# Scaled value copies of an attention kernel: made once per layer and loaded again, instead of made in every unit

## The chip, the cores and the metric

The kernel runs on one core of one Trainium2 chip. The metric is the time of one execution on the device in microseconds (us), as the median of several runs. The engines are called PE (matrix multiplication), ACT, DVE and POOL; SP issues the transfers between DRAM and the on-chip memory. PEld is the loading of weights into PE, which overlaps the matmuls.

## The reference

The program is a four-layer transformer stack on 2048 tokens of width 512: attention, MLP, attention, MLP, with the same weights in both attentions and in both MLPs. Attention has 32 heads of width 16.

```python
def _A_ref(x, wqkv, wo):                      # H = 32, Dh = 16
    q, k, v = split(x @ wqkv)
    p = softmax(einsum("bhqd,bhkd->bhqk", q, k) * Dh ** -0.5)
    return einsum("bhqk,bhkd->bhqd", p, v).merge_heads() @ wo
def _B_ref(x, w1, b1, w2, b2):                # F = 1376
    return gelu(layernorm(x) @ w1 + b1) @ w2 + b2
x = A_x
x = x + _A_ref(layernorm(x), A_wqkv, A_wo)
x = x + _B_ref(layernorm(x), B_w1, B_b1, B_w2, B_b2)
x = x + _A_ref(layernorm(x), A_wqkv, A_wo)
x = x + _B_ref(layernorm(x), B_w1, B_b1, B_w2, B_b2)
```

Everything is bfloat16 at the boundary.

## The kernel before

**Segments.** The code numbers the two attention layers L = 1 and L = 3. A layer is cut into units of 512 queries (in L = 3 the last unit is cut in two of 256), and a unit into 8 head groups (`hg`) of 4 heads. One unit and one head group make a *segment*; a segment's keys and values are 16 blocks of 128 tokens. The first unit of a layer starts before all keys are there, so its segments exist twice, as part 0 and part 1 (`nparts == 2`): key blocks 0 to 3 and 4 to 15 in L = 1, 0 to 11 and 12 to 15 in L = 3. All later units have `nparts == 1` and see all 16 blocks. That makes 32 segments with two parts and 56 with one, 88 in all.

**Two ways to an exponential.** A score tile is 128 keys by 512 queries, made on PE by `score` (L1354). In the usual way ACT takes two or three tiles at once from PSUM and writes their exponentials to `PT` (L1339). For the key blocks in `DK = (3, 6, 9, 12, 15)` there is a second way, the *d tile*: DVE copies the scores to 16-bit integers whose bits are read as bfloat16, an approximate exponential (L1431, `d_load`), and then makes three copies of two such tiles at a time, shifted by 32, 64 and 96 (L1462, `job_d`). The four versions are multiplied with four differently scaled versions of the values, so that the errors of the approximation average out. The scaled values are `vs`, three copies of the value blocks multiplied by `WSHIFT[1..3]`; the fourth is the unscaled `V`. So an ACT tile costs one value matmul on PE (L1528) and a d tile costs four. A value matmul has 17 columns (16 values and a one for the softmax's denominator); four heads run side by side in PE's columns.

**Where vs comes from.** `vs` has three slots. A segment takes a slot together with its query slot (`qt`, three of them), and once its queries are scaled (L1116, `job_qt`) `job_vs` is started. It has POOL multiply the segment's value blocks by the three constants, three instructions in a row (L1131), and then marks the blocks as usable. `take_d` gives out a d tile only when its block is marked. The slot is free again once the value matmuls of the segment that had it are done.

**Who decides the order.** The program is written out by a list scheduler in Python: jobs are generators that hand over tasks with a priority, and the scheduler keeps a modelled time for each engine and each resource and gives each engine the task that can start first. The model's durations stand in the code (the last numbers of each `I(...)`). The result is one fixed instruction list per engine, with semaphore waits between them. Whether a score tile goes to ACT or DVE is decided while this list is made: `take_d` gives a tile to DVE when DVE's modelled backlog and the free PSUM banks allow, and the others go to ACT. At the end `refill` puts matmuls with zeros into PE's modelled gaps (L1263, L1265, L1267). All transfers are issued on SP, in the order of its list, each with its own waits: the transposed load of a segment's queries (`qraw`, L1103), the transposes of the layernormed rows (`xnT`, `yT`) and of the attention output (`OT`), weights and stores.

**The side work.** Between the segments' instructions lie those of the layernorms, projections and MLPs of other units (`job_lnqkv`, `job_post`, `job_ffn`); POOL computes the inverse roots of the layernorms and merges the two parts of a split segment.

Of the kernel before, what the change touches and what calls it, by code (L numbers as in the profile page):

```python
# [8 lines left out]
BF16 = mybir.dt.bfloat16  # L9
# [29 lines left out]
DK = (3, 6, 9, 12, 15)  # L39
# [458 lines left out]
class Builder:  # L498
# [16 lines left out]
    def build_segments(self):  # L515
        self.segs = []
        four = [tuple(range(4 * c, 4 * c + 4)) for c in range(self.NC)]
        self.units = {1: four, 3: four[:3] + [four[3][:2], four[3][2:]]}
        for L in (1, 3):
            parts = [tuple(range(0, 4)), tuple(range(4, 16))] if L == 1 else [tuple(range(0, 12)), tuple(range(12, 16))]  # L520
            for pi in range(2):
                for hg in range(8):
                    self.segs.append(dict(L=L, qc=0, hg=hg, part=pi, nparts=2, kbs=parts[pi]))
            for qc in range(1, len(self.units[L])):
                for hg in range(8):
                    self.segs.append(dict(L=L, qc=qc, hg=hg, part=1, nparts=1, kbs=tuple(range(16))))
        for i, sg in enumerate(self.segs):
            sg["i"] = i
            sg["toks"] = self.units[sg["L"]][sg["qc"]]
            sg["W"] = 128 * len(sg["toks"])  # L530
            g = 512 // sg["W"]
            sg["dks"] = [kb for kb in sg["kbs"] if kb in DK]
            kbs = list(sg["kbs"]) if g == 1 else [kb for kb in sg["kbs"] if kb not in DK] + sg["dks"]
            sg["tiles"] = [(tuple(kbs[k:k + g]), hp) for k in range(0, len(kbs), g) for hp in range(4)]
            sg["nt"] = sg["n"] = len(sg["tiles"])
            sg["todo"] = [j for j, t in enumerate(sg["tiles"]) if not set(t[0]) <= set(DK)]
            sg["todod"] = [j for j, t in enumerate(sg["tiles"]) if set(t[0]) <= set(DK)]
            sg["rdy"] = []
            sg["sub"] = 0
            sg["emitted"] = 0  # L540
            sg["first"] = set()

    def alloc(self, es):
        nc = self.nc
        S, NT, NC, NFC = self.S, self.NT, self.NC, self.NFC
        t = lambda name, shape, dt: es.enter_context(nc.sbuf_tensor(name, shape, dt))
        self.xres = t("xres", [128, NT, 512], BF16)
        self.wqkv = t("wqkv", [128, 4, 1536], BF16)
        self.wo = t("wo", [128, 4, 512], BF16)
        self.wf = t("wf", [128, NFC, 512], BF16)  # L550
        self.bst = t("bst", [32, 128], BF16)
        self.b1c = t("b1c", [128, NFC], F32)
        self.ident = t("ident", [128, 128], BF16)
        self.zw = t("zw", [128, FILL_MOST], BF16)
        self.iog = t("iog", [128, 4], F32)
        self.iogt = t("iogt", [128, 4], F32)
        self.ioe = t("ioe", [32, 8, 4], F32)
        self.mask8 = t("mask8", [32, 8], F32)
        self.m4 = t("m4", [32, 4], F32)
        self.sel = t("sel", [32, 128], BF16)  # L560
        self.onesm = t("onesm", [128, 1], F32)
        self.row16 = t("row16", [128, 1], F32)
        self.qbias = t("qbias", [128, 1], F32)
        self.cneg = t("cneg", [128, 4], F32)
        self.chalf = t("chalf", [128, 1], F32)
        self.xnT = t("xnT", [128, 3, 4, 128], BF16)
        self.qk = t("qk", [128, 2, 2, 1024], BF16)
        self.vst = t("vst", [128, 1, 544], BF16)
        self.KT = t("KT", [128, 8, S], BF16)
        self.V = t("V", [128, 8, NT, 4, 17], BF16)  # L570
        self.qraw = t("qraw", [128, 2, 512], BF16)
        self.QT = t("QT", [128, 3, 512], BF16)
        self.PT = t("PT", [128, 23, 512], BF16)
        self.dp = t("dp", [128, NDP, 1024], U16)
        self.vs = t("vs", [128, 3, 3, len(DK), 68], BF16)
        self.OT = t("OT", [128, 8, 512], BF16)
        self.accT = t("accT", [128, 2, 512], F32)
        self.ob = t("ob", [128, 16, 8, 16], BF16)
        self.obl = t("obl", [128, 256], BF16)
        self.rv = t("rv", [128, 2, 16], F32)  # L580
        self.rowA = t("rowA", [128, 8, 16], BF16)
        self.dw = t("dw", [128, 2, 16], F32)
        self.den = t("den", [128, 8, 16], F32)
        self.yT = t("yT", [128, 4, 512], BF16)
        self.h16 = t("h16", [128, NFC, 512], BF16)
        self.g10 = t("g10", [128, 512], BF16)
        self.xn = t("xn", [128, 3, 512], BF16)
        self.sq0 = t("sq", [128, 1024], BF16)
        self.n2 = t("n2", [128, 4, 32], F32)
        self.n2k = t("n2k", [128, NT + 1, 32], BF16)  # L590
        self.nm = t("nm", [128, 32], BF16)
        self.qy = t("qy", [128, 4, 32], I32)
        self.qt1 = t("qt1", [128, 4, 32], F32)
        self.qt2 = t("qt2", [128, 4, 32], F32)
        self.kmx = t("kmx", [32, 4], F32)
        self.krhs = t("krhs", [32, 8], BF16)
        self.scl = t("scl", [128, 4, 8], F32)
        self.st = t("st", [128, 8, 6], F32)
        self.mv = t("mv", [128, 16, 2], F32)
        self.rs = t("rs", [128, 16], F32)  # L600
        self.ioi = self.dp[:, 6, 0:256].bitcast(F32)
        self.gv = self.h16[:, :, :].rearrange("p f n -> p (f n)")
        self.sbuf_left = nc.sbuf_bytes_remaining
        self.ps = es.enter_context(nc.psum_tensor("ps", [128, 8, 512], F32))
        self.q_scr = nc.dram_tensor("q_scr", [2, S, 1024], BF16, kind="Internal").ap()
        self.k_scr = nc.dram_tensor("k_scr", [S, 1024], BF16, kind="Internal").ap()
        self.v_scr = nc.dram_tensor("v_scr", [S, 544], BF16, kind="Internal").ap()
        self.sems = {}
        for e in list(ENGINES) + ["dma%d" % i for i in range(NDMAQ)]:
            self.sems[e] = es.enter_context(nc.semaphore("s_" + e))  # L610
        pl = self.S_.pools
        pl["mb"] = Pool([7, 5, 4, 3, 2, 1, 0])
        pl["pt3"] = Pool([0, 3, 6, 13, 18])
        pl["pt2"] = Pool([9, 11, 16, 21])
        pl["dp"] = Pool(range(8))
        pl["qraw"] = Pool(range(2))
        pl["qt"] = Pool(range(3))
        pl["qk"] = Pool(range(3))
        pl["vst"] = Pool([])
        pl["xn"] = Pool(range(3))  # L620
        pl["xnT"] = Pool(range(3))
        pl["sq"] = Pool(range(4))
        pl["n2"] = Pool(range(4))
        pl["accT"] = Pool(range(2))
        pl["st"] = Pool(range(8))
        pl["lnc"] = Pool(range(4))
        pl["kmx"] = Pool(range(1))
# [498 lines left out]
    def job_vs(self, sg, i, kbs):  # L1126

        q, hg, n = sg["qslot"], sg["hg"], len(kbs)
        yield ("keys", self.kv_keys(sg, kbs))
        src = self.V[:, hg, kbs[0]:kbs[-1] + 1:3, :, :].rearrange("p k h d -> p k (h d)")  # L1130
        yield Task("pool", 0.8, [I(lambda e, k=k: e.tensor_scalar(out=self.vs[:, q, k - 1, i:i + n, :], in0=src, scalar1=WSHIFT[k], scalar2=None, op0=ALU.mult),  # L1131
                                   [("V", hg, kb) for kb in kbs], [("vs", q, i + k2) for k2 in range(n)], 0.209 + 0.17 * n, [("vs", q, i + k2) for k2 in range(n)] if k > 1 else []) for k in (1, 2, 3)])
        for kb in kbs:
            self.S_.mark(("vs", sg["i"], kb))

    def job_kload(self, hg):

# [316 lines left out]
    def job_d(self, bt):  # L1454
# [4 lines left out]
        for k in range(1, len(SHIFT)):  # L1459
            v = yield ("get", "dp", sg["i"])  # L1460
            pr = 0.15 if not self.left(sg) and sg is self.segs[self.acc_seg] else 0.5 if self.left(sg) < DURGE else 2.5
            yield Task("dve", pr, [I(lambda e, k=k, v=v: e.tensor_scalar(out=self.dp[:, v, 0:N], in0=self.dp[:, u, 0:N], scalar1=float(SHIFT[k]), scalar2=None, op0=ALU.add),  # L1462
                                     [("dp", u, w) for w in range(n)], [("dp", v, w) for w in range(n)] + self.dres(v), 0.163 + 0.2605e-3 * N)])
            self.d_ready(bt, k, v, range(n))
        self.flying -= 1
        self.use_done(("dp", u))
# [12 lines left out]
    def try_pv(self):  # L1479
        S_ = self.S_  # L1480
        while True:
# [35 lines left out]
            for (s_, j, res, ap, use, sh) in pick:  # L1517
# [3 lines left out]
                sg["first"].add(hp)  # L1521
                for i, kb in enumerate(kbs):
                    if sh:
                        d = sg["dks"].index(kb)
                        v, RV = self.vs[:, q, sh - 1, d, 17 * hp:17 * hp + 17], ("vs", q, d)
                    else:
                        v, RV = self.V[:, hg, kb, hp, :], ("V", hg, kb)
# [361 lines left out]
```

## Time and profile before

| | |
|---|---|
| median of 5 runs | 1620.59 us (1618.09 to 1621.5) |
| profiled execution, its own time | 1618.09 us |
| its span (first to last instruction) | 1616.3 us |
| PE, ACT, DVE, POOL busy | 1577.8, 1548.3, 1471.6, 380.6 us |
| L1339, exponentials on ACT | 1470.0 us |
| L1431 and L1462, d tiles on DVE | 600.1 and 527.8 us |
| L1131, scaled values on POOL | 242.9 us in 240 instructions |

A row of the groups names the line, the engine, the operation, what it writes and reads, and the count; then its busy time and the mean duration of one in ns; then the idle time of the engine just before these instructions and what ended most of it. Busy time counts what overlaps once, so it can be less than count times mean. The chain that ended last is followed back from the last instruction, at each step to what released it. Matmuls are pipelined and their ends are modelled, so that a busy PE is not a PE at its peak.

### The profile page before, as it was taken

Reading aid. Unit: us, or ns where it says so; the run is one execution under the profiler, and the core shown is the slowest. Engines: PE = TensorE matmul, PEld = TensorE weight load, DVE = VectorE, ACT = ScalarE, POOL = GpSimd, SP = SyncE. Lnnn points to the kernel's source line nnn. Section 1 sums busy time; section 2 is a strip of 40 time slices with the busy share of each in tenths; the row PEclk is TensorE's granted clock in tenths of the full one; section 3 lists DMA queues with packets and bytes.
Section 4 is the critical chain, followed back from the end, with each engine's and each line's share of the span. In section 5 each row is a group of like instructions: output and inputs, shape, how many; then the busy total and the mean of one; then the engine's idle time right before and its main releaser. Section 6 shows DMA issues by size and latency. Waiting matters only on the chain.

```text
span 1616.3 us, 38868 instructions
## 1 busy us (share of the span) xinstructions
PE 1577.8 (98%) x16349; PEld 482.4 (30%) x16349; DVE 1471.6 (91%) x3249; ACT 1548.3 (96%) x1375; POOL 380.6 (24%) x574
## 2 busy tenths in 40 slices
PE   9999999999999999999999999999999999999998
PEld 3222222222222222232222222222222222344454
DVE  7899999989998899989999899999889979999794
ACT  6999999999999999999999989999999999999996
POOL 4354241011211121112111135511111101223210
PEclk9999999999999999999999999999999999999999
DMA  6651001102211221222722230100001000100100
GB/s 175 118 125 61 9 11 24 44 14 62 77 31 30 52 67 28 50 45 76 123 38 54 59 89 21 31 19 8 14 11 21 21 16 4 20 20 7 27 11 21
DMA packets 196849, 69.98 MB, mean 43 GB/s; under 512 B 176412, under 2 KB 191041, under 8 KB 196673
## 3 DMA queue, kind: packets, MB, share of 16 engines
q1 hardware_dynamic: 196672, 67.49, 18.8%
q8 instruction: 128, 2.10, 0.5%
q14 instruction: 49, 0.39, 0.1%
HBM read 20.03 MB, written 15.30 MB: 22 GB/s over the span
## 4 chain that ended last, share of the span: by engine, by line
PE 52%; ACT 25%; DVE 19%; issue 2%; POOL 1%; DMA 1%; SPq 0%; POOLq 0%; DVEq 0%
ACT PT L1339 23%; PE ps L1354 18%; PE ps L1528 14%; DVE dp L1431 7%; DVE dp L1462 5%; PE ps L1707 4%; PE ps L1669 4%; PE ps L1263 3%; PE ps L900 3%; ACT h L1699 1%; DVE accT L1558 1%; PE ps L1267 1%; PE ps L1265 1%; PE ps L1614 1%; DVE QT L1116 1%
## 5 line engine op out<-in xcount | busy, mean ns | idle before, releaser
L1339 ACT ACTIVATE PT<-ps 128x1024 bf16<-128x1024 f32 (+1 forms) x1292 | 1470.0, 1262 | 41.7 <-PE ps L1354 35.3
L1354 PE MATMUL ps<-QT,KT 32*128 32x512 bf16 (+1 forms) x4608 | 675.5, 358 | 17.4 <-DVE dp L1431 7.9
L1431 DVE TENSOR_SCALAR dp<-ps 128x512 uint16<-128x512 f32 x898 | 600.1, 679 | 65.4 <-PE ps L1354 61.4
L1462 DVE TENSOR_SCALAR dp<-dp 128x1024 uint16<-128x1024 uint16 x1359 | 527.8, 429 | 11.0 <-PE ps L1528 6.2
L1528 PE MATMUL ps<-PT,V 128*17 128x512 bf16 (+1 forms) x3594 | 475.8, 358 | 0.2 <-ACT PT L1339 0.2
L1131 POOL TENSOR_SCALAR vs<-V 128x340 bf16<-128x340 bf16 (+3 forms) x240 | 242.9, 1012 | 845.6 <-PE ps L1528 776.8
L1528 PE MATMUL ps<-dp,vs 128*17 128x512 bf16 (+1 forms) x3042 | 434.4, 356 | 0.1
L1354 PEld LDWEIGHTS ps<-QT,KT 32*128 32x128 bf16 x4608 | 171.2, 91 | 547.7 <-ACT PT L1339 256.4
L1528 PE MATMUL ps<-dp,V 128*17 128x512 bf16 (+1 forms) x1014 | 211.5, 357 | 4.5 <-DVE accT L1558 3.0
L1265 PE MATMUL ps<-zw 32*128 32x444 bf16 (+2 forms) x718 | 194.7, 324 | 0.0
L1263 PE MATMUL ps<-zw 128*128 128x448 bf16 (+14 forms) x610 | 144.9, 334 | 2.7 <-DVE ps L709 1.7
L1528 PEld LDWEIGHTS ps<-dp,vs 128*17 128x17 bf16 x3042 | 111.3, 88 | 118.8 <-issue 97.5
L1528 PEld LDWEIGHTS ps<-PT,V 128*17 128x17 bf16 x3594 | 113.8, 88 | 107.4 <-issue 96.4
L1267 PE MATMUL ps<-zw 128*32 128x448 bf16 (+14 forms) x1462 | 141.4, 326 | 0.3
L1669 PE MATMUL ps<-yT,wf 128*128 128x512 bf16 (+3 forms) x396 | 103.3, 360 | 1.0 <-DVE yT L1790 0.5
L900 PE MATMUL ps<-wqkv,xnT 128*128 128x512 bf16 x336 | 92.7, 382 | 1.8 <-DVE h L913 0.6
L1263 PEld LDWEIGHTS ps<-zw 128*128 128x128 bf16 x610 | 46.8, 98 | 92.1 <-issue 59.5
L1528 PEld LDWEIGHTS ps<-dp,V 128*17 128x17 bf16 x1014 | 50.5, 88 | 53.5 <-issue 26.3
L1558 DVE STREAM_TRANSPOSE accT<-ps 128x512 f32<-128x512 f32 (+1 forms) x88 | 57.9, 658 | 7.8 <-PE ps L1528 6.1
L1693 DVE TENSOR_SCALAR h<-ps,b1c 128x512 bf16<-128x512 f32 (+2 forms) x88 | 62.0, 705 | 3.1 <-PE ps L1669 2.5
L1267 PEld LDWEIGHTS ps<-zw 128*32 128x32 bf16 x1462 | 50.7, 95 | 21.4 <-DVE dp L1431 3.0
L1265 PEld LDWEIGHTS ps<-zw 32*128 32x128 bf16 x718 | 54.1, 92 | 1.2
(172 smaller groups left out, 851.5 us busy)
## 6 DMA issues: line engine op xcount, KB each, us to landing
wf<-in_B_w_dram SPq DMA_DIRECT2D x90, 128.0 KB, 2.9
q_scr<-qk SPq DMA_DIRECT2D x22, 256.0 KB, 2.1
k_scr<-qk SPq DMA_DIRECT2D x12, 256.0 KB, 2.0
out_dram<-xres SPq DMA_DIRECT2D x16, 128.0 KB, 1.7
xres<-in_A_x_dram SPq DMA_DIRECT2D x7, 256.0 KB, 3.5
v_scr<-vst SPq DMA_DIRECT2D x12, 136.0 KB, 1.9
V<-v_scr SPq DMA_DIRECT2D x8, 204.0 KB, 5.0
wqkv<-in_A_wqkv_dram SPq DMA_DIRECT2D x3, 512.0 KB, 5.3
```

The source lines that it names most:

```text
L900: yield Task("pe", prio, [I(lambda e, c=c: e.matmul(self.ps[:, b, :], lhsT=xnT[:, c, :], rhs=self.wqkv[:, c, which * 512:which * 512 + 512 ...
L1131: yield Task("pool", 0.8, [I(lambda e, k=k: e.tensor_scalar(out=self.vs[:, q, k - 1, i:i + n, :], in0=src, scalar1=WSHIFT[k], scalar2=None ...
L1263: fn = lambda e: e.matmul(self.ps[:, b, 0:w], lhsT=self.zw[:, 0:128], rhs=self.zw[:, 0:w], start=st, stop=st, skip_group_check=True)
L1265: fn = lambda e: e.matmul(self.ps[:, b, 0:w], lhsT=self.zw[32 * p:32 * p + 32, 0:128], rhs=self.zw[32 * p:32 * p + 32, 0:w], start=st, sto ...
L1267: fn = lambda e: e.matmul(self.ps[32 * p:32 * p + 32, b, 0:w], lhsT=self.zw[:, 0:32], rhs=self.zw[:, 0:w], start=st, stop=st, skip_group_c ...
L1339: S_.submit(Task("act", 1e-5 * gi, [I(lambda e, pt=pt, n=n, b0=b0: e.activation(out=self.PT[:, pt:pt + n, :], in_=self.ps[:, b0:b0 + n, :] ...
L1354: return [I(lambda e, kb=kb, i=i: e.matmul(self.ps[:, b, i * W:(i + 1) * W], lhsT=self.KT[32 * hp:32 * hp + 32, hg, kb * 128:(kb + 1) * 12 ...
L1431: self.S_.submit(Task("dve", 0.0, [I(lambda e: e.tensor_scalar(out=self.dp[:, u, w * 512:(w + 1) * 512], in0=self.ps[:, b, :], scalar1=BIT ...
L1462: yield Task("dve", pr, [I(lambda e, k=k, v=v: e.tensor_scalar(out=self.dp[:, v, 0:N], in0=self.dp[:, u, 0:N], scalar1=float(SHIFT[k]), sc ...
L1528: ops.append((nth[j, sh] + 0.1 * i, I(lambda e, hp=hp, v=v, ap=ap[:, i * W:(i + 1) * W], first=first and i == 0, W=W: e.matmul(self.ps[32 ...
L1558: yield Task("dve", 0.3, [I(lambda e: e.transpose(self.accT[:, a, 0:W], self.ps[:, ACCB, 0:W]), [("ps", ACCB)], [RA], 0.17 + 0.535 * W / 5 ...
L1669: yield Task("pe", pr, [I(lambda e, c=c: e.matmul(self.ps[0:M, b, off:off + W], lhsT=self.w1(fc, c), rhs=self.yT[:, c, 0:W], start=(c == 0 ...
```

## The change

The scaled values of a layer and head group are the same for all its units. After the change the segments of the first unit make them on POOL, as before, and store them to a new DRAM tensor `vs_scr`; the 56 later segments load their slot from there, in one transfer of 128 rows of 2040 bytes (3 copies, 5 blocks, 68 values, 2 bytes), and POOL makes none for them. In L = 1 the second part of the first unit now scales all five blocks in `DK`, not only its own four, so that the stored copy is complete; `doff` shifts its index by one. In L = 3 the two parts store three and two blocks. The key `vsst` holds a load back until the store has been issued. Besides, the modelled duration of L1462 goes from 0.163 to 0.150 us plus the same slope.

```diff
+        self.vs_scr = nc.dram_tensor("vs_scr", [2, 8, 128, 3, len(DK), 68], BF16, kind="Internal").ap()
...
     def job_vs(self, sg, i, kbs):
 
         q, hg, n = sg["qslot"], sg["hg"], len(kbs)
+        L = sg["L"]
+        if sg["nparts"] == 1:
+            yield ("keys", [("vsst", L, hg)])
+            yield self.dma(lambda e: e.dma_start(self.vs[:, q, :, :, :], self.vs_scr[L // 2, hg]), [("vsscr", L, hg, 0), ("vsscr", L, hg, 1)], [("vs", q, k) for k in range(len(DK))], 0.8, 0.4, (2.0, 1.05))
+            for kb in kbs:
+                self.S_.mark(("vs", sg["i"], kb))
+            return
+        if L == 1:
+            kbs, n = list(DK), len(DK)
+            sg["doff"] = 1
         yield ("keys", self.kv_keys(sg, kbs))
...
         for kb in kbs:
             self.S_.mark(("vs", sg["i"], kb))
+        d = DK.index(kbs[0])
+        part = sg["part"] if L == 3 else 0
+        W = [("vsscr", L, hg, 0), ("vsscr", L, hg, 1)] if L == 1 else [("vsscr", L, hg, part)]
+        yield self.dma(lambda e: e.dma_start(self.vs_scr[L // 2, hg, :, :, d:d + n, :], self.vs[:, q, :, i:i + n, :]), [("vs", q, i + k2) for k2 in range(n)], W, 2.0, 0.4, (2.0, 1.05))
+        if L == 1 or part == 1:
+            self.S_.mark(("vsst", L, hg))
...
             yield Task("dve", pr, [I(lambda e, k=k, v=v: e.tensor_scalar(out=self.dp[:, v, 0:N], in0=self.dp[:, u, 0:N], scalar1=float(SHIFT[k]), scalar2=None, op0=ALU.add),
-                                     [("dp", u, w) for w in range(n)], [("dp", v, w) for w in range(n)] + self.dres(v), 0.163 + 0.2605e-3 * N)])
+                                     [("dp", u, w) for w in range(n)], [("dp", v, w) for w in range(n)] + self.dres(v), 0.150 + 0.2605e-3 * N)])
...
-                        d = sg["dks"].index(kb)
+                        d = sg["dks"].index(kb) + sg["doff"]
```

(`doff` is set to 0 for every segment in `build_segments`.)

## The prediction

> **What bounds the kernel now.** I read the page's busy shares and chain first, then the costliest groups, then the groups kept apart by shape.
>
> ```profile
> PE 1577.8 (98%) x16349; PEld 482.4 (30%) x16349; DVE 1471.6 (91%) x3249; ACT 1548.3 (96%) x1375; POOL 380.6 (24%) x574
> ...
> PE 52%; ACT 25%; DVE 19%; issue 2%; POOL 1%; DMA 1%; SPq 0%; POOLq 0%; DVEq 0%
> ...
> L1339 ACT ACTIVATE PT<-ps 128x1024 bf16<-128x1024 f32 (+1 forms) x1292 | 1470.0, 1262 | 41.7 <-PE ps L1354 35.3
> ...
> L1431 DVE TENSOR_SCALAR dp<-ps 128x512 uint16<-128x512 f32 x898 | 600.1, 679 | 65.4 <-PE ps L1354 61.4
> L1462 DVE TENSOR_SCALAR dp<-dp 128x1024 uint16<-128x1024 uint16 x1359 | 527.8, 429 | 11.0 <-PE ps L1528 6.2
> ```
>
> ACT is nearly full with one job, the exponentials of L1339. PE looks fuller still, but its zero-operand filler matmuls (L1263, L1265, L1267) are 144.9, 194.7 and 141.4 us of its groups' busy time: 481 us that can make room. DVE carries the other way of making an exponential, the d tiles (L1431 and L1462). So the score tiles are split between two full engines. By the shapes, ACT takes 614 x 3 + 678 x 2 = 3198 tiles and DVE 898. A tile costs ACT 1470.0 / 3198 = 0.460 us and DVE (600.1 + 527.8) / 898 = 1.256 us. POOL is 24% busy and holds 1% of the chain: its time as such is not what the kernel waits for. What POOL does to DVE is the question.
>
> ```profile
> L1131 POOL TENSOR_SCALAR vs<-V 128x340 bf16<-128x340 bf16 x168 | 184.9, 1101 | 705.8 <-PE ps L1528 648.8 <-PE ps L1267 49.7
> L1131 POOL TENSOR_SCALAR vs<-V 128x272 bf16<-128x272 bf16 x24 | 22.4, 932 | 26.5 <-PE ps L1528 25.2
> ```
>
> The change touches these groups, by shape. The 168 five-block scalings are those of the 56 segments that see all 16 key blocks; each waits in POOL for its slot's last readers on PE.
>
> ```profile
> L1462 DVE TENSOR_SCALAR dp<-dp x1359: 271/417/955, 93.8 to 1587.9; 128x1024 uint16<-128x1024 uint16 x190, 128x512 uint16<-128x512 uint16 x5
> ```
>
> The answer for source line L1462 gives minimum, median and maximum. The median is 417 ns, but the mean above is 429 and the longest 955: a few copies are stretched a great deal. Two stretches of the timeline, DVE and then POOL, show where:
>
> ```profile
> 1015.02 1.01 DVE L1462 TENSOR_SCALAR dp<-dp 128x1024 uint16<-128x1024 uint16 x2
> ...
> 1016.56 0.60 DVE L1462 TENSOR_SCALAR dp<-dp 128x1024 uint16<-128x1024 uint16 x1
> ```
>
> ```profile
> 1013.90 3.58 POOL L1131 TENSOR_SCALAR vs<-V 128x340 bf16<-128x340 bf16 x3
> ```
>
> The pair at 1015.02 and the copy at 1016.56 lie inside POOL's three scalings. Matching all 1335 full-size copies with POOL's records: 1068 meet no POOL work and take 415 ns, 142 meet a scaling and take 536 ns. The windows by stage say the same; this is L1462 in three stretches (us of DVE, count, clock, DMA share, GB/s):
>
> ```profile
> 960.00:1000.00 40.00, 14.46 (x38) 1.00 0.18 49
> 1000.00:1040.00 40.00, 17.61 (x36) 1.00 0.10 23
> 760.00:800.00 40.00, 14.78 (x39) 1.00 0.81 133
> ```
>
> In 1000 to 1040 us, where POOL scales for 14.8 us, a copy occupies 17.61 / 36 = 489 ns (overlap with its neighbours counted once). In 760 to 800, with 81% of the DMA engines' time taken and 5.5 us of scalings, it is 379: DMA traffic does not slow DVE here, POOL does.
>
> **Part 1: 168 scalings go.** Their own 184.9 us on POOL are worth nothing directly: POOL's chain share is 1%. What they did to DVE is worth something. Summing, over all DVE operations that overlap one of the 168, the duration beyond that of the same operation met by no POOL work gives 19.4 us: most of it on L1462, and some on L1116 (QT, 394 ns alone, 482 beside a scaling), L1600 and L843. The 8 first-layer segments that scale four blocks now scale five: 24 scalings grow from 932 to 1101 ns, 4 us of POOL and at the same rate (19.4 / 184.9) 0.4 us of DVE. So DVE gets back 19.0 us.
>
> The Trainium skill, SBUF — State Buffer, section "SBUF: two separate sides", says that DVE in some modes and GpSimd take one shared port pair as an exclusive lock for a whole instruction, and that the loser fully blocks. By that, a DVE copy meeting a scaling would wait about half of 1101 ns; 168 such waits would be an estimated 92 us, and the gain worked out below some 34 us. The trace agrees on who meets whom and not on the amount (142 copies lose 121 ns each), so the rows decide.
>
> **Part 2: the cost constant of L1462** falls from 0.163 to 0.150 us plus the same slope: 0.430 becomes 0.417 for 1024 elements. It changes no instruction's duration. It changes the order that the scheduler writes out, which then believes in 1335 x 0.013 = 17.4 us less DVE work. That nearly equals the 19.0 us that really go, so order and chip still fit; the admission rule in take_d (it looks at DVE's backlog) lets in more d tiles.
>
> **What 19.0 us of DVE are worth.** If all of it is filled with d tiles: 19.0 / 1.256 = 15 tiles, and ACT loses 15 x 0.460 = 6.9 us. PE pays three more value matmuls a tile, four side by side at 382 ns: 15 x 0.29 = 4.3 us, hidden in the 481 us of filler; without that cover the gain would shrink to 2.6. If none is filled and only the stretched operations lying on the chain count, it is DVE's chain share: 19.0 x 0.19 = 3.6 us. DVE's 145 us of idle time, 61.4 of them waiting for scores, speak for the lower value; ACT's 96% speaks for the higher. I take the middle, 5.3 us. Late next is ACT again, and at unit ends the scores of PE.
>
> **Part 3: 56 loads and 24 stores on SP's queue.** A load moves 128 x 2040 bytes, 255 KB. No such load is in the trace; the nearest rows are these, in KB and microseconds to landing:
>
> ```profile
> q_scr<-qk SPq DMA_DIRECT2D x22, 256.0 KB, 2.1
> xres<-in_A_x_dram SPq DMA_DIRECT2D x7, 256.0 KB, 3.5
> V<-v_scr SPq DMA_DIRECT2D x8, 204.0 KB, 5.0
> ```
>
> I take 3 us, near the first two, whose rows are as long; 5.0 is the far end, with 136-byte pieces. A slot comes free two segments before its next use (about 24 us each from 200 to 1400 us, about 12 us after that), and the scalings took 3 x 1.1 = 3.3 us themselves, so the load's own length is covered; without that cover it would be 3 us per segment. The wait for the slot's readers, which POOL bore in its 60 waits, now stands on SP, and what SP holds behind it is the next qraw transpose (landing 2.6 us, needed a segment later) and now and then an xnT, yT or OT transpose of the side work: 40 + 30 + 36 = 106 of them. With a load every 29 us, a tenth of these meet one and wait half of it, 11 x 1.5 = 16 us in all. DMA holds 1% of the chain, 16 us, of their 106 x 2.6 = 276 us: 6%. So 1.0 us lands on the path. Ends: a gain of 1, because POOL's layernorm steps no longer queue behind three scalings; a loss of 4.4, the longest DMA step of the chain (v_scr, 4.37 us at the change of layer) met once more. The stores come after scalings that nobody waits for longer than now; they cost nothing, or are part of that same end.
>
> **Sum.** -5.3 + 1.0 = -4.3 us. The profiled execution took 1618.09 us around a span of 1616.3; it would take 1613.8. It is the lowest of the five runs and the median lies 2.5 above it, so the median goes from 1620.59 to 1616.3, or -0.27%. About 0.2% (3.2 us) is what a measurement of this kernel can tell from no change.
>
> **Rivals.**
> ACT starves (slower). Every instruction's place is recomputed, and ACT already idles 41.7 us before its exponentials, 35.3 of them in 78 waits for scores, 0.45 us each. More d tiles put more value matmuls ahead of score groups in PE's in-order queue. One more average wait in every fourth of the 88 segments is 22 x 0.45 = 9.9 us: -4.3 + 9.9 = +5.6, 1626.2. It decides once the idle time before L1339 passes 46. Against it: the filler on PE. For it: ACT has nothing else to do in such a gap.
> DVE keeps the relief (no change). The d tiles stay near 898, DVE's idle time before L1431 grows from 65.4 towards 84, and the 1.0 us of DMA is all that is left: 1621.6. For it: the 61.4 us in which DVE waits for scores. Against: 91% busy, and 12 to 15 d tiles in most segments where 20 would be allowed.
> The copies come late: loads land after the first d tile needs them, 3 us in 56 segments at the worst, 168 us; at one segment in ten +17, 1638. Against it stand the two segments of lead.
>
> **How the numbers follow.** Forecast 0.58, of which 0.06 lies within 0.2%; no change 0.12; ACT starves 0.28; late copies 0.02. So faster 0.52, same 0.18, slower 0.30. The range runs from 1606 (all 6.9 us, and a fifth of the 38.6 us that PE's weight loads wait for L1462: -14.6) to 1627 (ACT starves, 1626.2, rounded up); about 2 in 10 is left outside: late copies, a deeper starvation, a better order. The forecast's own range is 1606 to 1618.
>
> **What would show it.** Right: L1131 at 72, L1462's mean at 415 to 420 and its median unchanged, 905 to 915 d tiles, ACT's exponentials about 1463 us busy. Wrong: idle time before L1339 above 46 us, d tiles at 898 or fewer, L1462's mean still near 429, or PE waiting for a DMA into vs.

## The result, and the profile after

The changed kernel takes 1622.79 us in the median of 29 runs, the kernel before 1620.87 in the median of 51: a ratio of 1.0019, interval 1.0013 to 1.0026. It is slower by 0.2%, just at the edge of what can be told from no change; forecast was 1616.3. The profiled execution took 1622.63 us around a span of 1620.8, at a granted TensorE clock of 0.998 (1 is full clock throughout). Before's was one of its quicker runs, at 1.0, so the two spans (1616.3 and 1620.8) lie further apart than the medians. The clock does not make the difference: the runs of both kernels with a granted clock of 0.998 average 1622.4 us after (7 runs) and 1620.6 before (16 runs, of those made with the experiments).

The page after: busy shares and chain, then the groups that answer to those shown of before (names of lines have moved by 18: L1339 is now L1357, L1431 L1449, L1462 L1480; L1131 is L1143).

```profile
PE 1583.1 (98%) x16531; PEld 482.2 (30%) x16531; DVE 1463.5 (90%) x3283; ACT 1539.4 (95%) x1369; POOL 194.9 (12%) x406
...
PE 44%; ACT 31%; DVE 22%; issue 2%; POOL 1%; DMA 0%; POOLq 0%; DVEq 0%
...
L1357 ACT ACTIVATE PT<-ps 128x1024 bf16<-128x1024 f32 (+1 forms) x1288 | 1463.8, 1273 | 44.2 <-PE ps L1372 39.1
...
L1449 DVE TENSOR_SCALAR dp<-ps 128x512 uint16<-128x512 f32 x908 | 607.7, 679 | 66.0 <-PE ps L1372 61.6
L1480 DVE TENSOR_SCALAR dp<-dp 128x1024 uint16<-128x1024 uint16 (+1 forms) x1383 | 523.4, 420 | 8.4 <-PE ps L1546 3.9
...
L1143 POOL TENSOR_SCALAR vs<-V 128x340 bf16<-128x340 bf16 (+2 forms) x72 | 61.4, 853 | 141.8 <-PE ps L1546 138.2
...
vs<-vs_scr SPq DMA_DIRECT2D x56, 255.0 KB, 2.7
```

Every local sign that the prediction called right has come: 72 scalings, copies at 420 ns instead of 429, 908 d tiles instead of 898, 6 us less of exponentials. The loads land in 2.7 us, no engine waits for one, and none is in the chain, whose DMA steps round to 0%. Only the time did not follow. The end of the program shows why. These are the last two places where the segments' work and the MLP work finish, in the timeline of before: the last transposed sum of a segment on DVE, then the last row that DVE writes for the next-to-last unit's MLP and the large Gelu on ACT that needs it, with the last eleven exponentials:

```profile
1595.94 0.45 DVE L1558 STREAM_TRANSPOSE accT<-ps 128x256 f32<-128x256 f32 x1 [1.40 <-PE ps L1528]
```

```profile
1575.32 0.47 DVE L1693 TENSOR_SCALAR h<-ps,b1c 96x256 bf16<-96x256 f32 x1
```

```profile
1578.46 2.34 ACT L1699 ACTIVATE h<-h 128x2560 bf16<-128x2560 bf16 x1
...
1582.56 12.50 ACT L1339 ACTIVATE PT<-ps 128x1024 bf16<-128x1024 f32 x11
```

and in the timeline after, with the wait of the closing MLP's first Gelu:

```profile
1587.55 0.45 DVE L1576 STREAM_TRANSPOSE accT<-ps 128x256 f32<-128x256 f32 x1 [1.80 <-PE ps L1546]
```

```profile
1585.27 0.48 DVE L1711 TENSOR_SCALAR h<-ps,b1c 96x256 bf16<-96x256 f32 x1 [1.19 <-PE ps L1687]
```

```profile
1573.98 12.49 ACT L1357 ACTIVATE PT<-ps 128x1024 bf16<-128x1024 f32 x11
...
1587.78 2.34 ACT L1717 ACTIVATE h<-h 128x2560 bf16<-128x2560 bf16 x1
```

```profile
ACT h L1779 <- PE ps L1687: 21.4, 4, 17.7
```

The segments finish 8.4 us earlier than before: their stream did get shorter. But the Gelu of the next-to-last unit's MLP comes 9.3 us later, because its input comes 10 us later (the rows of L1693 and L1711). In ACT's list the last eleven exponentials now stand before this Gelu and no longer behind it, and the closing unit (`job_tail`) waits for that MLP. Before, its work after the last scores took 1616.3 - 1595.9 = 20.4 us; now it begins only after the MLP, and the last Gelu is 1620.8 - 1587.8 = 33.0 us from the end. ACT stands idle for 17.7 us at a stretch in between (7.2 before). These two distances gave a rule to test: the span ends at the later of *last transposed sum + 20.4* and *last large Gelu + 33.0*.

### The profile page after: what moved, and what is told of

It reads as the page before. It is cut to its first block, busy times and chain, and to the rows that moved or that the text cites. A ratio compares the mean times of both kernels' runs of the same rounds, so it can differ in the third digit from the quotient of the medians.

```text
span 1620.8 us, 39194 instructions
## 1 busy us (share of the span) xinstructions
PE 1583.1 (98%) x16531; PEld 482.2 (30%) x16531; DVE 1463.5 (90%) x3283; ACT 1539.4 (95%) x1369; POOL 194.9 (12%) x406
## 4 chain that ended last, share of the span: by engine, by line
PE 44%; ACT 31%; DVE 22%; issue 2%; POOL 1%; DMA 0%; POOLq 0%; DVEq 0%
ACT PT L1357 28%; PE ps L1372 15%; PE ps L1546 12%; DVE dp L1449 8%; DVE dp L1480 6%; PE ps L1725 4%; PE ps L1687 4%; PE ps L902 3%; PE ps L1281 3%; ACT h L1717 2%; DVE accT L1576 1%; PE ps L1632 1%; DVE st L832 1%; PE ps L1283 1%; PE ps L1018 1%
## 5 line engine op out<-in xcount | busy, mean ns | idle before, releaser
L1357 ACT ACTIVATE PT<-ps 128x1024 bf16<-128x1024 f32 (+1 forms) x1288 | 1463.8, 1273 | 44.2 <-PE ps L1372 39.1
L1449 DVE TENSOR_SCALAR dp<-ps 128x512 uint16<-128x512 f32 x908 | 607.7, 679 | 66.0 <-PE ps L1372 61.6
L1480 DVE TENSOR_SCALAR dp<-dp 128x1024 uint16<-128x1024 uint16 (+1 forms) x1383 | 523.4, 420 | 8.4 <-PE ps L1546 3.9
L1546 PE MATMUL ps<-PT,V 128*17 128x512 bf16 (+1 forms) x3583 | 470.0, 359 | 1.1 <-DVE accT L1576 1.1
L1283 PE MATMUL ps<-zw 32*128 32x444 bf16 (+2 forms) x814 | 223.7, 324 | 0.0
L1546 PE MATMUL ps<-dp,V 128*17 128x512 bf16 (+1 forms) x1025 | 205.3, 358 | 3.0 <-DVE accT L1576 2.7
L1285 PE MATMUL ps<-zw 128*32 128x448 bf16 (+17 forms) x1552 | 149.6, 325 | 0.6 <-DVE accT L1576 0.6
L1281 PE MATMUL ps<-zw 128*128 128x448 bf16 (+22 forms) x573 | 138.0, 337 | 4.0 <-DVE ps L711 1.7
L1143 POOL TENSOR_SCALAR vs<-V 128x340 bf16<-128x340 bf16 (+2 forms) x72 | 61.4, 853 | 141.8 <-PE ps L1546 138.2
L1711 DVE TENSOR_SCALAR h<-ps,b1c 128x512 bf16<-128x512 f32 (+2 forms) x88 | 61.7, 702 | 7.1 <-PE ps L1687 6.9
L1283 PEld LDWEIGHTS ps<-zw 32*128 32x128 bf16 x814 | 61.3, 92 | 1.6
```

What stands on the lines that cost most here:

```text
L1281: fn = lambda e: e.matmul(self.ps[:, b, 0:w], lhsT=self.zw[:, 0:128], rhs=self.zw[:, 0:w], start=st, stop=st, skip_group_check=True)
L1283: fn = lambda e: e.matmul(self.ps[:, b, 0:w], lhsT=self.zw[32 * p:32 * p + 32, 0:128], rhs=self.zw[32 * p:32 * p + 32, 0:w], start=st, sto ...
L1285: fn = lambda e: e.matmul(self.ps[32 * p:32 * p + 32, b, 0:w], lhsT=self.zw[:, 0:32], rhs=self.zw[:, 0:w], start=st, stop=st, skip_group_c ...
L1357: S_.submit(Task("act", 1e-5 * gi, [I(lambda e, pt=pt, n=n, b0=b0: e.activation(out=self.PT[:, pt:pt + n, :], in_=self.ps[:, b0:b0 + n, :] ...
L1449: self.S_.submit(Task("dve", 0.0, [I(lambda e: e.tensor_scalar(out=self.dp[:, u, w * 512:(w + 1) * 512], in0=self.ps[:, b, :], scalar1=BIT ...
L1546: ops.append((nth[j, sh] + 0.1 * i, I(lambda e, hp=hp, v=v, ap=ap[:, i * W:(i + 1) * W], first=first and i == 0, W=W: e.matmul(self.ps[32 ...
```

## The experiments

Two theories at first. A: the end is decided by the recomputed order, by that rule. B: the loads cost what the relief gives; and, beside it, C: the half-clock stretches do. "Before" below is the kernel before on the same chip, 1620.6 to 1621.4 us in the three sets.

**Old constant, with the loads** (`0.150` back to `0.163`).

> The changed kernel with the modelled duration of the DVE copies put back to 0.163 us; the loads stay. Theory A (the end is set by the order: the last full segment's transposed sum on DVE plus 20.4 us, or the last Gelu activation plus 33.0 us, whichever is later; both offsets are read from the two traces): the order is a new one, so the time may lie 10 us to either side of before, but the span must be that maximum within 1.5 us, and loads are not what it waits for. Rival B (the 56 loads cost time on SP's and the DMA queue): still slower than before by 2 us or more, with DMA or SP entries in the chain. Rival C (half-clock stretches of PE cost the gain): time follows the granted clock, about 1.2 us for each 0.001, and nothing else.

1620.17 us, ratio 1.0008 (0.9996 to 1.0019): no change. Span 1617.0 at clock 1.0, again set by the MLP: last Gelu 1584.0 + 33.0. C falls as the whole cause: the clock is full and the gain is still not there. Over 69 runs of before the granted clock itself lay between 0.997 and 1.0, with a median of 0.998 against 0.997 in the runs of the changed kernel; the time goes up by 1.4 us for each 0.001 that is missing, so a median also carries the clocks of its runs. At full clock this kernel is 1.4 us slower than before (1619.2 in 7 runs, 1617.8 in 19). B is not decided by this run.

**The constant alone, no loads** (`0.163` to `0.150` in the kernel before).

> The kernel before with only the modelled duration of the DVE copies lowered from 0.163 to 0.150 us; no loads, no stores, all 240 scalings on POOL. Theory A: again a new order; the scores end earlier, as in the changed kernel (by 5 to 12 us), and the span is the later of scores plus 20.4 and Gelu plus 33.0, within 1.5 us; little or no gain over before. Rival B: without loads the whole gain appears: 5 us or more faster than before. Rival C: as B if the clock stays at 1.0, otherwise 1.2 us less for each 0.001 of clock.

1630.83 us, ratio 1.0077 (1.0058 to 1.0095): 10.0 us slower. A asked for little or no gain and had the direction of the scores right, 3.2 us earlier instead of 5 to 12; the size of the loss it did not foresee. The rule holds (Gelu 1593.4 + 33.0 = 1626.4, the span). B's expectation is refuted: there are no loads here, and the time is the worst so far.

**The relief alone, in before's order:**

```diff
+        def scale(e, k):
+            if sg["nparts"] == 1:
+                return e.tensor_scalar(out=self.vs[:, q, k - 1, 4, 0:1], in0=self.V[:, hg, 15, 0, 0:1], scalar1=WSHIFT[k], scalar2=None, op0=ALU.mult)
...
-        yield Task("pool", 0.8, [I(lambda e, k=k: e.tensor_scalar(out=self.vs[:, q, k - 1, i:i + n, :], in0=src, scalar1=WSHIFT[k], scalar2=None, op0=ALU.mult),
+        yield Task("pool", 0.8, [I(lambda e, k=k: scale(e, k),
```

> The kernel before with every instruction in its place, but in the 56 later segments POOL's three scalings write one element each instead of 340, so the scaled values of those segments are stale: this leaves that part of the computation out. It removes POOL's disturbance of DVE and nothing else. The prediction's sum for relief that is not filled with new tiles: -3.6 us (DVE's share of the chain, 0.19 of 19.0 us). Theory A: between 0 and -4 us, the copies' mean falling from 429 to 417-420 ns. Rival: a fixed order absorbs it all, 0 within 1 us, because the copies that were stretched had slack and ACT stays full.

1610.16 us, ratio 0.9938 (0.9926 to 0.9950): 10.6 us faster in the median, three times the expected 3.6. All five runs had a clock of 0.999 or 1.0, where only 20 of before's 69 did. At full clock it is 1610.0 (4 runs) against 1617.8 (19 runs): 7.8 us, still twice the 3.6. Whether the relief itself keeps the clock up was not tried. Its busy shares, to hold against those of before:

```profile
PE 1574.8 (98%) x16349; PEld 481.1 (30%) x16349; DVE 1457.6 (91%) x3249; ACT 1546.1 (96%) x1375; POOL 234.4 (15%) x575
```

DVE lost 14.0 us of work (1471.6 to 1457.6) and ACT 2.2, while no tile moved (898 d tiles in both). At full clock the time went down by a little over half of DVE's relief. The waits fit this: ACT's idle time before its exponentials fell from 41.7 to 36.0 us, and PE's weight loads for scores waited 56.4 us for a d tile's bank instead of 67.5.

**The changed kernel with the last MLP ahead:**

```diff
-        return 0.95 if L == 1 and qc >= self.NC - 2 else 2.2
+        return 0.95 if L == 1 and qc >= self.NC - 2 or L == 3 and qc >= 3 else 2.2
```

> The changed kernel with one more edit: the attention output and MLP of layer 3 from its fourth unit on get priority 0.95 instead of 2.2, so that they go before the value matmuls. Theory A: the last Gelu moves from 1587.8 us to 1573 or earlier, the end is set by the scores again, and the span falls from 1620.8 to 1608-1614, faster than before by 3 us or more. Rival B (the loads cost the time) and rival C (the clock does): no more than 2 us less than the changed kernel.

1617.60 us, ratio 0.9974 (0.9962 to 0.9986), 5.2 us less than the changed kernel. The Gelu moved from 1587.8 to 1569.7, and the end went over to the scores:

```profile
1591.44 0.45 DVE L1576 STREAM_TRANSPOSE accT<-ps 128x256 f32<-128x256 f32 x1 [4.83 <-PE ps L1546]
```

1591.4 + 20.4 = 1611.8 against a span of 1612.3. The scores paid 3.9 us for it. So the late MLP was what the changed kernel ended on.

**2 ns of the constant** (`0.150` to `0.148`). From here theory D: the chip pays for the order, and for how far DVE's real durations lie from those the order was made with; loads cost nothing. Rival E: the change has a cost of its own.

> The changed kernel with the modelled duration of the DVE copies at 0.148 instead of 0.150 us: 2 ns, no other edit. Theory D (the hardware pays for two things only: where the recomputed order puts the last scores and the last MLP, and how far DVE's real durations lie from the modelled ones; loads and stores cost nothing): a new order, so the time may differ from the changed kernel by several us in spite of the 2 ns; this value was picked because the scheduler's own sum for it ends early, so 8 us or more faster than the changed kernel, span 1604-1612, and again the later of last transposed sum plus 20.4 and last Gelu plus 33.0. Rival E (the change has a cost of its own that any order must bear): within 2 us of the changed kernel, 1621-1625.

1608.54 us, ratio 0.9932 (0.9920 to 0.9943): 14 us below the changed kernel, for 2 ns in a number that no instruction knows. E's 1621 to 1625 is missed by far.

**The same constant, without loads:**

> The kernel before (all 240 scalings on POOL, no loads) with the modelled duration at 0.148 us. Theory D: an early order too, but DVE is 13-15 ns slower per copy than modelled, as in the run with the constant alone; against the changed kernel with 0.148 it is slower by 5 to 12 us, the worth of POOL's silence. Rival E: against the changed kernel with 0.148 it is equal or faster, since it bears no loads.

1620.74 us, ratio 1.0001 (0.9991 to 1.0012): 12.2 us more than with the loads, just outside D's 5 to 12. It ends on the scores (1598.2 + 20.4 = 1618.6; span 1618.5).

**More loads**, a second load after each of the 56:

```diff
+        self.vdum = t("vdum", [128, 2, 5, 68], BF16)
...
+            if op.eng == "sp" and any(r[0] == "vsscr" for r in op.reads):
+                _, L, hg, _ = op.reads[0]
+                P.op("sp", lambda e, L=L, hg=hg: e.dma_start(self.vdum[:, :, :, :], self.vs_scr[L // 2, hg, :, 0:2, :, :]), op.reads, [("vdum",)], (), 0.0, (0.0, 0.0))
```

> The changed kernel with every instruction in its place and after each of the 56 loads a second one of two of the three copies (174 KB) into a tile that nobody reads. It adds 9.7 MB of traffic and 56 issues on SP's queue. Theory D: no change against the changed kernel, within 1.5 us. Rival E (loads cost): slower by about two thirds of what the 56 loads cost, 5 us or more if they ate the gain.

1623.48 us, ratio 1.0024 (1.0015 to 1.0033) where the changed kernel has 1.0019 (1.0013 to 1.0026): no difference that the intervals show, so that the loads' traffic costs little or nothing. These second loads wait for what the first had already waited for. What the first ones hold up on SP is read from the trace instead: PE waits 4.8 us in all for scaled queries in the changed kernel, 4.9 in before, and no engine waits longer than 0.9 us for a transfer.

**The scalings given back to the changed order**, on constant data, started by each segment's scaled queries:

```diff
+        self.vdum = t("vdum", [128, 2, 340], BF16)
...
+            if op.eng == "sp" and any(r[0] == "vsscr" for r in op.reads):
+                qd = max((o for o in P.streams["dve"] if any(r[0] == "qt" for r in o.writes)), key=lambda o: o.pos).writes[0]
+                for m_ in (1, 2, 3):
+                    P.op("pool", lambda e, m_=m_: e.tensor_scalar(out=self.vdum[:, m_ % 2, :], in0=self.zw[:, 0:340], scalar1=WSHIFT[m_], scalar2=None, op0=ALU.mult), [qd, ("zw",)], [("vdum", m_ % 2)], (), 0.0)
```

> The changed kernel with every instruction in its place, and POOL again does three 340-element scalings in each of the 56 later segments, started by the segment's scaled queries, from constant data into a tile that nobody reads. It gives POOL's disturbance of DVE back to the new order. Theory D: slower than the changed kernel by 6 to 11 us, copies at 430 ns. Rival: within 2 us, if the changed order has slack where the scalings fall.

1657.25 us, ratio 1.0236 (1.0218 to 1.0254): 34.5 us slower than the changed kernel, three times what D expected. Its groups:

```profile
L1362 ACT ACTIVATE PT<-ps 128x1024 bf16<-128x1024 f32 (+1 forms) x1288 | 1472.0, 1255 | 69.9 <-PE ps L1377 62.9
...
L1485 DVE TENSOR_SCALAR dp<-dp 128x1024 uint16<-128x1024 uint16 (+1 forms) x1383 | 556.5, 444 | 9.5 <-PE ps L1551 5.4
...
L1272 POOL TENSOR_SCALAR vdum<-zw 128x340 bf16<-128x340 bf16 x168 | 191.9, 1142 | 789.6 <-DVE QT L1119 753.6
```

The copies are at 444 ns, and ACT's idle time before the exponentials rose from 44.2 to 69.9 us. Started right behind the scaled queries, the scalings of this kernel (240 with the 72 that it had) meet 222 full-size copies and take them to 581 ns, 36.9 us more than at 415; in before, 240 scalings met 142 at 536 ns, 17.2 us more. That is 32 us more of stretching than in the changed kernel (4.9); DVE's whole busy time rose by 37.1 us (1463.5 to 1500.6). Its four runs had clocks of 0.989 to 0.996; against runs of the changed kernel at 0.993, 0.995 and 0.996 it is about 30 us slower, four fifths of what DVE got more to do. Not all of this need come through DVE: POOL's own steps now queue behind the scalings, DVE's idle time that POOL ends is 11.1 us instead of 4.7, and the scalings themselves hold 1% of the chain. Why this place is worse than where POOL scaled before was not tried.

**0.158 and 0.177**, the changed kernel otherwise. F, beside D: the true duration is the right value and only the order of 0.150 was unlucky.

> The changed kernel with the modelled duration of the DVE copies at 0.158 us. Theory D: one more new order; the value was picked because the scheduler's own sum for it ends earliest of those tried, and it also lies 8 ns above the quiet copies' real duration, which so far made the chip finish ahead of the order. 15 us or more faster than before, span 1600-1606, last transposed sum plus 20.4 or last Gelu plus 33.0. Rival F (0.150 is the right value and only that order was unlucky): no better than the run with 0.148, 1608.5.

> The changed kernel with the modelled duration at 0.177 us, 27 ns above the quiet copies' real duration. Theory D: the chip finishes further ahead of the order, but fewer tiles are admitted; faster than before by 10 us or more, span 1598-1608. Rival F (the model should be true): slower than with 0.150, 1623 or more, because DVE is held to be busier than it is and ACT gets more tiles.

1601.66 us, ratio 0.9883 (0.9867 to 0.9899), and 1614.46 us, ratio 0.9947 (0.9926 to 0.9967). The first is 19.8 us faster than before and the fastest kernel of this study, with a span (1598.6) a little below D's range. The second is far from F's 1623 and in the median short of D's 10 us; four of its six runs, the profiled one among them, had a clock of 0.994, and the two at 0.999 and 1.0 took 1606.9 and 1608.0 us, 10 less than before at full clock. In the first both ends are early:

```profile
1578.01 0.45 DVE L1576 STREAM_TRANSPOSE accT<-ps 128x256 f32<-128x256 f32 x1 [1.93 <-PE ps L1546]
```

```profile
1563.82 2.34 ACT L1717 ACTIVATE h<-h 128x2560 bf16<-128x2560 bf16 x1
```

**Relief in the order of the constant alone** (the edit of the third experiment with 0.150).

> The kernel with the constant alone at 0.150 us (1630.8 us), every instruction in its place, but in the 56 later segments POOL's scalings write one element each, so the scaled values of those segments are stale: this leaves that part of the computation out. It has the relief and the new constant, without loads. Theory D: 8 to 13 us faster than 1630.8, so 1618 to 1623, about the changed kernel's time: the constant's order eats what the relief gives. Rival E (the loads cost): clearly below the changed kernel, 1615 or less.

1620.21 us, ratio 0.9996 (0.9985 to 1.0008): 10.6 us faster than 1630.83 in the median. That this is the same 10.6 as in before's order is chance, because the clocks differ. Runs at 0.998 give a clean account from before to after:

| kernel | runs at clock 0.998 | mean, us | step, us |
|---|---|---|---|
| before | 16 | 1620.6 | |
| constant alone | 3 | 1630.5 | +9.9 |
| relief, 0.150 | 5 | 1618.1 | -12.4 |
| after | 7 | 1622.4 | +4.3 |

The first step is a new order, the second the relief in a fixed order, the third the real loads and stores in yet another order. DVE lost 23.5 us of work by the relief here (1488.3 to 1464.8), so again a little over half of it reaches the time. With the relief the constant costs 10 us by the medians (1610.16 to 1620.21), but no runs of like clock are there to compare; taking 1.4 us off for each 0.001 of clock leaves some 5, an estimate. E's 1615 is missed.

**Before with the last MLP ahead**, the control of the fourth experiment.

> The kernel before with layer 3's last attention outputs and MLP at priority 0.95, the edit that took 5 us off the changed kernel. Theory A: before's end is set by the scores (1595.9 + 20.4 against 1578.5 + 33.0), so there is nothing to gain: within 2 us of before, with the last Gelu earlier by 5 us or more. Rival: the edit is good by itself, for any order: 4 us or more faster than before.

1621.31 us, ratio 0.9998 (0.9989 to 1.0006): no change, though the Gelu moved from 1578.5 to 1566.8. Before ends on the scores, so moving the MLP gives nothing: the sums come 3.9 us later instead.

**The rule over all profiles** (us; the two offsets were read from the first two rows, the other rows test them):

| kernel | last sum | last Gelu | rule | span |
|---|---|---|---|---|
| before | 1595.9 | 1578.5 | 1616.3 | 1616.3 |
| after | 1587.5 | 1587.8 | 1620.8 | 1620.8 |
| old constant, loads | 1592.0 | 1584.0 | 1617.0 | 1617.0 |
| constant alone | 1592.7 | 1593.4 | 1626.4 | 1626.4 |
| relief alone | 1588.5 | 1571.0 | 1608.9 | 1608.8 |
| after, MLP ahead | 1591.4 | 1569.7 | 1611.8 | 1612.3 |
| after, 0.148 | 1586.9 | 1559.9 | 1607.3 | 1607.5 |
| before, 0.148 | 1598.2 | 1581.0 | 1618.6 | 1618.5 |
| more loads | 1588.9 | 1589.1 | 1622.1 | 1622.1 |
| scalings back | 1621.7 | 1622.0 | 1655.0 | 1655.0 |
| after, 0.158 | 1578.0 | 1563.8 | 1598.4 | 1598.6 |
| after, 0.177 | 1594.0 | 1576.5 | 1614.4 | 1614.4 |
| relief, 0.150 | 1585.1 | 1585.8 | 1618.8 | 1618.9 |
| before, MLP ahead | 1599.8 | 1566.8 | 1620.2 | 1620.1 |

The traces also show what the late orders have in common. In the five rows with 0.150 whose end the Gelu sets, no exponential stands behind the last Gelu in ACT's list, and it starts within 0.7 us of the last sum. In the old constant with loads, which the Gelu also sets, three exponentials stand behind it. In the eight rows that end on the scores it is 8 to 25 (11 in before).

## Why the prediction was wrong, by its steps

**The relief** was put at 19.0 us of DVE. The relief alone took 14.0 us off DVE's busy time (its one-element scalings still occupy POOL for 39.5 us). In the order of 0.150 it was 23.5. Right in kind, and the size lies between the two. One reading was wrong: the longest copies of before (816 to 955 ns, eight of them) are not the scalings' work alone; each overlaps one of POOL's merges of a split segment, which the change keeps.

**What the relief is worth** was mis-sized. The prediction took 5.3 us, between DVE's chain share (3.6) and a full exchange for tiles (6.9). Measured in a fixed order and at like clock it is 7.8 us in before's order and 12.4 in that of 0.150, each a little over half of what DVE got back, where the prediction took 5.3 / 19.0, little more than a quarter; the reverse experiment lost more still. A chain share is the share of all of DVE's work that lies on the path of one execution. The reading that fits the waits, though no run tests it by itself: a stretched copy sits in a dense, fixed stream, delays the freeing of the bank that the next scores need, and so holds PE and then ACT.

**The constant and the new order** is the step that failed. The prediction said that order and chip would still fit and more tiles would be let in. The tiles came (898 to 908) and the scores ended early, but the lower constant cost 10.0 us by itself: its order places the last MLP late, the Gelu at 1593.4 us instead of 1578.5 and behind all exponentials, while its scores end 3 us earlier. In the changed kernel the profile shows the two running apart. From the end of segment 55 to that of segment 87 the sums go from 6.8 us behind before to 8.4 ahead, while the MLP work of the unit whose output transposes start at nearly the same time (1402.1 and 1402.8) falls behind: its Gelu is 4.2 us late, the next unit's 9.3. In the code the MLP has priority 2.2 on PE, behind the value matmuls (1.0); giving it 0.95 moved the end back to the scores. The prediction looked at what fills the engines and never asked which of two finishing lines sets the end. So the account of +1.9 us is, at a clock of 0.998: +9.9 for the order of the lower constant, -12.4 for the relief in it, +4.3 for the loads and their order. With the relief's worth in before's order, 7.8, the remainder for the order is some 10 us.

**The loads** were put at 1.0 us on the path, with ends of -1 and 4.4. As traffic they cost nothing that shows: 56 further ones added 0.7 us, inside the intervals. As an edit of the plan they are one more new order, and with the old constant that one cost more than the relief gave (1610.0 to 1619.2 us at full clock). That it is the order and not the loads is argued from the traffic run and the waits; no run keeps the order and takes the loads away.

**The rivals.** "ACT starves" had the sign, not the mechanism: idle time before the exponentials is 44.2 us, below its threshold of 46; the idle stretch came in the closing MLP. "DVE keeps the relief" and "the copies come late" did not happen. The range held the time, but by luck: its upper end stood for a starving ACT, and the time got there because two larger effects nearly cancelled. The direction was wrong.

**What stays open.** Five values of the constant with loads gave 1608.5, 1622.8, 1601.7, 1620.2 and 1614.5 us (0.148, 0.150, 0.158, 0.163, 0.177), and 0.148 and 0.158 were picked for an early end in the scheduler's own sum, so this is no fair sample. At equal constants the whole change was worth 12.2, 8.0 and 0.6 us (0.148, 0.150, 0.163), and the 0.6 turns into a loss of 1.4 at full clock. Why the scheduler puts the last MLP so late in one order and not in its neighbour was not taken apart. That the distance between modelled and real durations costs time beyond the order, as D says, was not shown.

The Trainium skill's rule on the shared port pair (SBUF — State Buffer, section "SBUF: two separate sides") finds who meets whom again. The prediction's estimate from it, half a scaling for each meeting, is again too large: even in the worst placement 222 meetings cost 166 ns each, not half of a scaling's 1142.

## What to carry to other kernels

When an edit makes a scheduler recompute its order, measure the two effects apart: first the edit's physical effect with every instruction left in its place, then the new order; here they were about -8 to -12 and about +10 to +14 us and cancelled. Compare runs of like clock, since a median mixes them. Before pricing relief on a busy engine, find which streams of work end last and by how much, since work that lets one stream run ahead can push the other past it. And a modelled duration is also a knob of the order: try its neighbours before judging the edit that came with it.

## What the runs showed of the hardware

A DVE copy of 415 ns (1024 elements) that overlaps a POOL scaling takes 536 ns on average in before, and one of 416 ns takes 581 with the scalings moved. Taking the scalings away in a fixed order shortened the time by a little over half of the busy time that DVE lost (7.8 of 14.0 us at full clock, 12.4 of 23.5 at 0.998). The records of the changed kernel's profiled run show PE at half clock in two stretches of 3.41 us within its span; those of other profiled runs, the very end of each left aside, are 3.41, 6.83, 10.24 or 20.48 us long. The Trainium skill, TensorE: Matmul & The Clock Gate, section "Part 1: The HAM clock gate", gives a free-running window of 3413 ns; the stretches agree. Over 69 runs of before, 0.001 of granted clock goes with 1.4 us.
